# Linear attention with a gated feed-forward on one core: q times k'v in four 64x64 quarters of the TensorE array

## The chip, the cores and the metric

One core of one Trainium2 chip. The metric is the device time of one execution in microseconds (us), lower is better; the time before is the median of three runs. Engines: PE is TensorE's matmul, PEld its weight loads (they overlap PE), DVE is VectorE, ACT ScalarE, POOL GpSimd, SP SyncE, which here only issues DMAs.

## What is computed

Eight batches, eight heads, 576 tokens, 64 channels a head. The attention is linear: softmax of q over its channels, softmax of k over the tokens, and the 64x64 product k'v in between; no score matrix. Behind it stands a gated layer over all 512 channels: a causal depthwise convolution of five taps makes the gate, a product with w_val makes the value, and gate times value goes through w_out. All in fp32.

```python
q_s = np.exp(q - np.max(q, axis=-1, keepdims=True))
q_s = q_s / (np.sum(q_s, axis=-1, keepdims=True) + 1e-09)
k_s = np.exp(k - np.max(k, axis=2, keepdims=True))
k_s = k_s / (np.sum(k_s, axis=2, keepdims=True) + 1e-09)
kv = np.einsum('bhsd,bhse->bhde', k_s, v)
x = np.einsum('bhsd,bhde->bhse', q_s, kv)          # then heads side by side: (8, 576, 512)
for j in range(5):
    gate_pre += conv_w[j] * xp[:, j:j + S, :]      # xp: x with four zero rows ahead
out = (1.0 / (1.0 + np.exp(-gate_pre)) * (x @ w_val)) @ w_out
```

## The kernel before, in words

The work goes batch by batch, and within a batch by *pairs of heads* p (128 channels, so 4 pairs) or by chunks of 128 tokens. A batch has these steps, each a small function:

- **q** (lines 357 to 397): q_max, q_sub, q_exp, q_sum, q_mul make the softmax with tokens on the partitions. In batches 0 and 1 q_each does the subtraction and the exponential per head on ScalarE for some chunks. q_turn (435) transposes q on TensorE, eight blocks of 128x128 into one PSUM buffer; q_turned (446) copies two pairs to the tile qT, with the channels of a pair on the partitions. The 64 tokens left over by the four chunks are turned for two batches together (tail_turn, tail_turned, tail_high, lines 458 to 470).
- **k** (278 to 350): the maximum over tokens comes from a second copy of k with channels on the partitions (k_peak, 283); it goes through DRAM (k_row, k_spread) to be spread over the partitions, then k_sub, k_exp, kt_exp. Batches 0 and 1 use k_top, k_raise and transposes (k_turn) instead.
- **k'v** (kv, 399): for each pair and each of five chunks of tokens one fp32 product per head, 128 tokens by 64 channels, into rows 0 to 63 or 64 to 127 of PSUM: the two heads use the two halves of the array's columns. kv_sums and kv_norm (414, 419) divide by the sums; kv_norm runs once per half and writes into the diagonal blocks of a 128x128 tile kvd whose other blocks are zero.
- **x = q times k'v** (attend, 476): per pair of heads one product over the full array, in two halves of 288 tokens. In batches 0 and 1 (F32_BATCHES) q and kvd are fp32. In the others they are split into high words (fp32r, a reduced format that TensorE takes in one pass) and low words: kv_high and kv_low (427, 431) split kvd, q_turned writes the high words of q, q_low and tail_low (454, 472) the low ones into the buffers "under"; attend then makes three products, low by high, high by high, high by low, in one accumulation.
- **the gated layer** (491 to 564): x_high and x_low split x the same way; first and four tap steps on VectorE form the gate from x in PSUM; a tap can instead be a far on ScalarE (the product) and a near on GpSimd (the addition). sigmoid, then value (546), 24 products over the full array for one block of 128 channels, gated, g_high, g_low, project (562), again 24 products, copy, put.

PSUM is four buffers of two banks each (psum, bank, 157), shared by all transposes, k'v, x, value and project; x of a pair stays in its buffer until its taps and x_low are done. At the start each slab of the two weights arrives as 64-bit words and is turned to fp32 by integer steps (load_words to w_low, lines 225 to 274).

What sets the order is the list ORDER (lines 30 to 143, 1011 steps), written out by hand: each engine, and SP's DMA queue, does its instructions in the order in which they stand there. A last letter a, v or p puts a step on ScalarE, VectorE or GpSimd. The buffers of a tag are taken in turn as they come free, so a load that stands early in the list waits on SP until its buffer is free, with all loads behind it.

## Time and profile before

| | us |
|---|---|
| median of 3 runs | 305.2 (304.4 to 305.86) |
| the profiled execution, its own time | 305.72 |
| its span in the profile | 303.9 |
| TensorE busy | 279.1 (92%) |
| VectorE busy | 255.5 (84%) |
| GpSimd busy | 220.4 (73%) |
| ScalarE busy | 216.2 (71%) |

A span is what the profile covers of one execution. Busy time counts an engine's instructions, overlaps once; TensorE's products are pipelined and their ends are modelled, so durations of single products are longer than their spacing, and the rate is read from how many start in a stretch. An fp32 product shows as two records, one pass with the low words of the weights and one with the high words; an fp32r product shows as one. The chain of waits follows the work that ended last back to what released each piece.

### The profile page before, as it was taken

How to read it: one execution, taken by the hardware profiler on the slowest of the kernel's cores; microseconds unless marked ns; L12 is line 12 of the kernel's file. 1: busy time of each engine (PE TensorE's matmuls, PEld its weight loads, DVE VectorE, ACT ScalarE, POOL GpSimd, SP SyncE). 2: the span in 40 equal slices, each digit the busy share in tenths (PEclk: the TensorE clock that was granted, in tenths of full speed). 3: DMA queues.
4: the chain of work that ended last, by engine and by line, in shares of the span. 5: the costliest groups of instructions: out<-in, count | busy, mean ns of one | idle time of the engine just before them, and what ended most of it. 6: DMA issues, size and time to landing. Idle time of an engine off the chain costs nothing.

```text
span 303.9 us, 6467 instructions
## 1 busy us (share of the span) xinstructions
PE 279.1 (92%) x2536; PEld 271.1 (89%) x2536; DVE 255.5 (84%) x350; ACT 216.2 (71%) x357; POOL 220.4 (73%) x206
## 2 busy tenths in 40 slices
PE   0347899999999899999999999999999999999995
PEld 0336699999989799999999999999998999999995
DVE  3999999999999798999999898999779876836611
ACT  3999999967795996869673964659496885464220
POOL 4677959799989699659787879784886949752500
PEclk9978999999999999999999999999999999999999
DMA  7999491389598822618597099023201210021012
GB/s 240 408 405 396 156 397 45 103 187 361 194 319 261 327 102 75 217 54 284 158 395 304 39 259 332 17 90 106 38 0 39 80 41 0 2 116 41 0 62 96
DMA packets 17454, 51.25 MB, mean 169 GB/s; under 512 B 2705, under 2 KB 3089, under 8 KB 14737
## 3 DMA queue, kind: packets, MB, share of 16 engines
q1 hardware_dynamic: 17424, 50.85, 47.9%
q8 instruction: 20, 0.33, 0.5%
q14 instruction: 10, 0.07, 0.1%
HBM read 41.39 MB, written 9.45 MB: 167 GB/s over the span
## 4 chain that ended last, share of the span: by engine, by line
PE 66%; ACT 11%; DVE 10%; DMA 7%; issue 2%; POOL 2%; SPq 1%; ACTq 0%; DVEq 0%
PE out L534 26%; PE val L534 25%; PE x L487 7%; PE kv L407 4%; PE qTps L439 3%; DVE qs L377 3%; DMA q<-in_q 3%; DMA words<-in_w_val 2%; ACT q L392 2%; DMA out<-o 2%; DVE qm L361 1%; ACT L523 1%; DVE qs L378 1%; ACT qT L171 1%; DVE gate L511 1%
## 5 line engine op out<-in xcount | busy, mean ns | idle before, releaser
L534 PE MATMUL val<-x,w_val_hi 128*128 128x288 f32 x512 | 88.4, 294 | 0.0
L534 PEld LDWEIGHTS val<-x,w_val_hi 128*128 128x128 f32 x512 | 74.8, 188 | 0.0
L511 DVE SCALAR_TENSOR_TENSOR gate<-x,cw,gate 128x573 f32<-128x573 f32 (+3 forms) x91 | 72.1, 807 | 2.2 <-ACT gate L500 1.2
L520 POOL TENSOR_TENSOR gate<-gate,far 128x572 f32<-128x572 f32 (+3 forms) x37 | 49.5, 1341 | 27.3 <-ACT far L516 26.4
L534 PE MATMUL out<-gh,w_out_lo 128*128 128x288 f32 x256 | 55.9, 297 | 1.1 <-ACT o L171 0.6
L534 PE MATMUL val<-x,w_val_lo 128*128 128x288 f32 x256 | 56.0, 299 | 0.0
L534 PE MATMUL out<-gh,w_out_hi 128*128 128x288 f32 x256 | 55.0, 294 | 0.0
L534 PEld LDWEIGHTS out<-gh,w_out_lo 128*128 128x128 f32 x256 | 41.2, 188 | 2.1 <-ACT o L171 0.9
L534 PEld LDWEIGHTS val<-x,w_val_lo 128*128 128x128 f32 x256 | 40.7, 188 | 0.7 <-DVE x L173 0.2
L534 PEld LDWEIGHTS out<-gh,w_out_hi 128*128 128x128 f32 x256 | 41.2, 188 | 0.0
L560 POOL TENSOR_TENSOR gl<-g,gh 128x576 fp32r<-128x576 f32 x24 | 34.6, 1449 | 7.2 <-ACT gh L171 5.0
L534 PE MATMUL out<-gl,w_out_hi 128*128 128x288 f32 x256 | 39.2, 294 | 0.0
L516 ACT ACTIVATE far<-x,cw 128x572 f32<-128x572 f32 (+3 forms) x37 | 27.0, 745 | 13.7 <-DVE gate L511 6.7
L534 PEld LDWEIGHTS out<-gl,w_out_hi 128*128 128x128 f32 x256 | 35.7, 188 | 0.0
L552 DVE TENSOR_TENSOR g<-val,gate 128x576 f32<-128x576 f32 x32 | 24.0, 751 | 10.0 <-PE val L534 5.8
L366 POOL TENSOR_TENSOR q<-q,qm 128x512 f32<-128x512 f32 x29 | 31.0, 1086 | 0.7 <-issue 0.7
L171 ACT COPY o<-out 128x576 f32<-128x576 f32 x27 | 17.2, 637 | 16.7 <-PE out L534 11.5
L301 POOL TENSOR_TENSOR k<-k,kmax 128x512 f32<-128x512 f32 x21 | 28.6, 1377 | 0.1
L506 DVE TENSOR_TENSOR x<-x,x 128x576 fp32r<-128x576 f32 x32 | 23.2, 747 | 6.3 <-ACT far L516 4.1
L523 ACT ACTIVATE gate<-gate 128x576 f32<-128x576 f32 x32 | 21.1, 685 | 8.4 <-DVE gate L511 5.4
L394 POOL TENSOR_TENSOR q<-q,qs 128x512 f32<-128x512 f32 x25 | 26.0, 1048 | 0.8 <-DVE qs L379 0.6
L500 ACT ACTIVATE gate<-x,cw 128x576 f32<-128x576 f32 x27 | 19.9, 747 | 6.8 <-PE x L487 5.2
(88 smaller groups left out, 522.1 us busy)
## 6 DMA issues: line engine op xcount, KB each, us to landing
out<-o SPq DMA_DIRECT2D x31, 288.0 KB, 2.2
v<-in_v SPq DMA_DIRECT2D x8, 1040.0 KB, 8.9
...
```

The source lines that it names most:

```text
L301: engine(e).tensor_sub(kk[r, cs], kk[r, cs], mx[r, cs])
L366: engine(e).tensor_tensor(qq, qq, m, op=ALU.add if b < 2 else ALU.subtract)
L394: engine(e).tensor_mul(qq, qq, s.unsqueeze(2).broadcast_to([P, H, D]))
L487: nc.tensor.matmul(T["x", b, p][:, cs], a, z[:, cs], start=(i == 0), stop=(i == len(parts) - 1))
L506: nc.vector.tensor_sub(xl, T["x", b, p], T["xh", b, p].bitcast(F32))
L511: nc.vector.scalar_tensor_tensor(out=a, in0=x, scalar=w, in1=a, op0=ALU.mult, op1=ALU.add)
L516: nc.scalar.activation(T["far", b, p, j], T["x", b, p][:, :S - n], AF.Copy, scale=cw[:, p, j:j + 1])
L520: nc.gpsimd.tensor_add(a, a, T["far", b, p, j])
L523: nc.scalar.activation(T["gate", b, p], T["gate", b, p], AF.Sigmoid)
L534: nc.tensor.matmul(ps[:, cs], a[:, kb, ms], z[:, cs], start=(i == 0), stop=(i == len(parts) - 1))
L552: nc.vector.tensor_mul(T["g", b, m], T["val", b, m], T["gate", b, m])
L560: engine(e).tensor_sub(T["gl", b, m], T["g", b, m], T["gh", b, m].bitcast(F32))
```

## The change

q times k'v is done in fp32 in all batches, per head, on a quarter of the array: 64 rows by 64 columns. A step attend b g takes two pairs of heads, so four heads, and two PSUM buffers; it makes eight products, one for each head and each half of the tokens, in such an order that four consecutive ones fall on the four quarters. So that this is possible, the heads of every odd pair are exchanged in q (on the host, where the inputs are laid out) and in kv (the line `hd = 2 * p + (h + p) % 2`). The tile kvd has no zero blocks any more, and kv_norm is one instruction for both halves. kv_high, kv_low, q_low and tail_low fall away. The addition of the epsilon and the reciprocal come out of q_sum as steps of their own, q_eps (on any engine) and q_rec. The buffers of tag "f" go from 3 to 6, and the two slabs of words that shared the buffers "under" get buffers "late".

ORDER is new in whole, 959 steps. By kind: attend 32 to 16, kv_norm 16 to 8, far and near 37 to 25 each, tap 91 to 103, q_low 12, tail_low 12, kv_high 6 and kv_low 6 to none, q_eps and q_rec 10 each new; all loads, transposes, value and project in the same number as before. Steps change engines too: g_low on GpSimd 24 to 19, q_turned on VectorE 3 to 6, q_sub on VectorE 3 to 6, g_high on VectorE 5 to 9, first on VectorE 5 to 8. The order of the first 100 steps or so is close to the old one; further on value and project of different blocks change places. Functions and an input that the diff adds but that no step uses (load_qc, q_total, q_log, l_turn, l_row, l_spread, l_sub, c_exp) are left out below, as is the list.

```diff
-KM = 3
-F32_BATCHES = (0, 1)
+STAGED = 6
...
-        place = ("under", 2) if i in (4, 5) else ("pair", 6)
+        place = ("late", 2) if i in (4, 5) else ("pair", 6)
...
-        s = T["qs", b][:, cs]
-        nc.vector.tensor_reduce(out=s, in_=qq, axis=AX.X, op=ALU.add)
-        nc.vector.tensor_scalar_add(s, s, EPS)
+        nc.vector.tensor_reduce(out=T["qs", b][:, cs], in_=qq, axis=AX.X, op=ALU.add)
+
+    def q_eps(b, c0, c1, e="v"):
+        s = T["qs", b][:, heads(b, c0, c1)[1]]
+        if e == "a":
+            nc.scalar.activation(s, s, AF.Copy, bias=EPS)
+        elif e == "p":
+            nc.gpsimd.tensor_scalar(s, s, EPS, 0.0, op0=ALU.add, op1=ALU.add)
+        else:
+            nc.vector.tensor_scalar_add(s, s, EPS)
+
+    def q_rec(b, c0, c1):
+        s = T["qs", b][:, heads(b, c0, c1)[1]]
         nc.vector.reciprocal(s, s)
...
-                    hd = 2 * p + h
+                    hd = 2 * p + (h + p) % 2
...
-    def kv_norm(b, h, e="v"):
-        acc, s, r = T["kv", b], T["ks", b], slice(h * D, (h + 1) * D)
+    def kv_norm(b, e="v"):
+        acc, s = T["kv", b], T["ks", b]
+        t = T["kvd", b] = small.tile([P, NB, D], F32, tag="kvd", name=f"kvd_{b}")
         if e == "v":
-            nc.vector.tensor_mul(kvd[b % 2][r, :, r], acc[r, :, :D], s[r].unsqueeze(2).broadcast_to([D, NB, D]))
+            nc.vector.tensor_mul(t, acc[:, :, :D], s.unsqueeze(2).broadcast_to([P, NB, D]))
         else:
             for p in range(NB):
-                nc.scalar.mul(kvd[b % 2][r, p, r], acc[r, p, :D], s[r, p:p + 1])
+                nc.scalar.mul(t[:, p], acc[:, p, :D], s[:, p:p + 1])
...
-            T["qT", b] = work.tile([P, NB, S], F32 if b in F32_BATCHES else F32R, tag="qT", name=f"qT_{b}")
+            T["qT", b] = work.tile([P, NB, S], F32, tag="qT", name=f"qT_{b}")
...
-    def attend(b, p):
-
-        T["x", b, p] = halved_bank(f"x_{b}_{p}")
-        qh = T["qT", b][:, p]
-        if b in F32_BATCHES:
-            parts = ((kvd[b % 2][:, p], qh),)
-        else:
-            hi, lo = (T["kvs", b][:, i, p * P:(p + 1) * P] for i in range(2))
-            parts = ((lo, qh), (hi, qh), (hi, T["qTlo", b, p // 2][:, p % 2]))
-        for i, (a, z) in enumerate(parts):
-            for cs in tokens("a"):
-                nc.tensor.matmul(T["x", b, p][:, cs], a, z[:, cs], start=(i == 0), stop=(i == len(parts) - 1))
+    def attend(b, g):
+
+        kvb, qb = T["kvd", b], T["qT", b]
+        for p in (2 * g, 2 * g + 1):
+            T["x", b, p] = halved_bank(f"x_{b}_{p}")
+        for z in range(2):
+            for h in range(2):
+                for p in (2 * g, 2 * g + 1):
+                    cs = tokens("a")[(z + h) % 2]
+                    i, o = (slice(y * D, (y + 1) * D) for y in (h, (h + p) % 2))
+                    nc.tensor.matmul(T["x", b, p][o, cs], kvb[i, p], qb[i, p, cs], start=True, stop=True)
...
-    kvd = [const.tile([P, NB, P], F32, tag=f"kvd{i}", name=f"kvd{i}") for i in range(2)]
+    lses = [const.tile([P, 64], F32, tag=f"lse{i}", name=f"lse{i}") for i in range(2)]
     ktz = [const.tile([P, C], F32, tag=f"ktz{i}", name=f"ktz{i}") for i in range(2)]
+    eps = const.tile([P, 1], F32, tag="eps", name="eps")
+    nc.gpsimd.memset(eps, EPS)
     nc.scalar.preload_act_table(AF.Exp)
-    for t in kvd + ktz:
+    for t in ktz + lses:
...
+    q = np.asarray(q)[:, [h ^ (h // 2 % 2) for h in range(H)]]
     (qm, qt), (km, kt), (vm, vt) = tokens(q), tokens(k), tokens(v)
```

## Rows read from the trace of the kernel before

**Rows 1.** The page: busy time of each engine, its share of the span and its instructions; and the granted TensorE clock in 40 slices of 7.6 us, in tenths of full speed.

```profile
PE 279.1 (92%) x2536; PEld 271.1 (89%) x2536; DVE 255.5 (84%) x350; ACT 216.2 (71%) x357; POOL 220.4 (73%) x206
PEclk9978999999999999999999999999999999999999
```

**Rows 2.** Busy time of each engine by stretch of the span, with the number of instructions in brackets, then the granted clock, the DMA engines' share and GB/s.

```profile
20.00:40.00 20.00, 15.90 (x213) 13.37 (x212) 19.54 (x37) 19.27 (x41) 15.18 (x16) 0.86 0.81 304
40.00:78.00 38.00, 38.00 (x285) 36.79 (x282) 37.17 (x50) 33.44 (x60) 32.94 (x28) 1.00 0.65 221
78.00:110.00 32.00, 30.43 (x286) 29.20 (x282) 29.71 (x40) 26.24 (x46) 27.17 (x25) 1.00 0.74 250
110.00:180.00 70.00, 70.00 (x716) 69.19 (x715) 65.95 (x88) 52.39 (x80) 57.76 (x55) 1.00 0.55 186
180.00:260.00 80.00, 79.30 (x726) 78.31 (x726) 69.02 (x91) 55.03 (x78) 60.52 (x54) 1.00 0.24 82
260.00:300.00 40.00, 39.96 (x303) 39.73 (x302) 18.98 (x27) 15.41 (x24) 14.49 (x13) 1.00 0.13 49
```

**Rows 3.** Pieces of the chain that ended last, in order of time: start, length, engine, tile, line, count.

```profile
36.40 1.24 PE x L487 x4
37.64 2.48 PE kv L407 x80
53.98 0.87 PE qTps L439 x8
54.85 1.94 PE x L487 x8
118.46 3.17 PE val L534 x24
121.63 0.79 PE x L487 x6
289.26 11.39 PE out L534 x84
300.68 0.46 DVE o L173
```

**Rows 4.** Groups of instructions with their shapes: the products of q and k'v (line 487). After the bar: busy us, mean ns of one, idle time of the engine before them and what ended it.

```profile
L487 PE MATMUL x<-qT,kvs 128*128 128x288 f32 x96 | 16.8, 296 | 0.8 <-ACT o L171 0.8
L487 PE MATMUL x<-qTlo,kvs 128*128 128x288 f32 x48 | 10.3, 297 | 0.2 <-DVE qTlo L456 0.2
L487 PE MATMUL x<-qT,kvd 128*128 128x288 f32 x32 | 9.1, 417 | 1.4 <-ACT k L171 0.8 <-ACT qT L171 0.5
```

**Rows 5.** The instructions in order of time, merged, at the start of k'v of batch 3 (line 407): one row of each of three answers, cut at 110.80, 110.88 and 110.91 us. Start, length, engine, line, operation, shapes, count.

```profile
110.78 0.28 PE L407 MATMUL kv<-v,k 128*64 128x65 f32 x2
110.78 0.20 PEld L407 LDWEIGHTS kv<-v,k 128*64 128x64 f32 x4 [0.16 <-POOL gate L520]
110.78 0.34 PE L407 MATMUL kv<-v,k 128*64 128x65 f32 x4
```

**Rows 6.** The same view, TensorE alone, around that k'v: the end of the value product before it, its last two fifths and the start of the value product behind it.

```profile
109.76 1.09 PE L534 MATMUL val<-x,w_val_hi 128*128 128x288 f32 x7
...
112.00 0.64 PE L407 MATMUL kv<-v,k 128*64 128x65 f32 x16
112.58 0.64 PE L407 MATMUL kv<-v,k 128*64 128x65 f32 x16
113.26 0.54 PE L534 MATMUL val<-x,w_val_lo 128*128 128x288 f32 x2
113.64 0.43 PE L534 MATMUL val<-x,w_val_hi 128*128 128x288 f32 x2
```

**Rows 7.** Groups of the page and of VectorE's own list: taps, subtractions for the low words of q, normalization of k'v, the addition of the epsilon. Columns as in group 4.

```profile
L511 DVE SCALAR_TENSOR_TENSOR gate<-x,cw,gate 128x573 f32<-128x573 f32 (+3 forms) x91 | 72.1, 807 | 2.2 <-ACT gate L500 1.2
L456 DVE TENSOR_TENSOR qTlo<-qTps,qT 128x1024 fp32r<-128x1024 f32 x12 | 14.4, 1218 | 2.7 <-ACT qT L171 2.6
L422 DVE TENSOR_TENSOR kvd<-kv,ks 64x256 f32<-64x256 f32 x13 | 5.5, 422 | 0.3
L378 DVE TENSOR_SCALAR qs<-qs 128x16 f32<-128x16 f32 (+3 forms) x10 | 4.9, 495 | 0.3
```

**Rows 8.** Groups of the page on GpSimd and ScalarE: gate additions, low words of g, and the products handed to GpSimd.

```profile
L520 POOL TENSOR_TENSOR gate<-gate,far 128x572 f32<-128x572 f32 (+3 forms) x37 | 49.5, 1341 | 27.3 <-ACT far L516 26.4
L560 POOL TENSOR_TENSOR gl<-g,gh 128x576 fp32r<-128x576 f32 x24 | 34.6, 1449 | 7.2 <-ACT gh L171 5.0
L516 ACT ACTIVATE far<-x,cw 128x572 f32<-128x572 f32 (+3 forms) x37 | 27.0, 745 | 13.7 <-DVE gate L511 6.7
```

**Rows 9.** The instructions in order of time: VectorE, the low words of x for two pairs of heads of batch 1; TensorE, the start of value 1 1.

```profile
68.89 1.54 DVE L506 TENSOR_TENSOR x<-x,x 128x576 fp32r<-128x576 f32 x2
...
71.29 0.42 PE L534 MATMUL val<-x,w_val_lo 128*128 128x288 f32 x2
```

**Rows 10.** Waits of TensorE, and of its weight loads: us in total, times, longest.

```profile
PE x L487 <- ACT o L171: 0.8, 1, 0.8
PE x L487 <- DVE qTlo L456: 0.2, 1, 0.2
PEld x L487 <- DVE qTlo L456: 0.5, 1, 0.5
```

More of the change, by code (lines that the diff above doesn't have):

```diff
@@ new lines @@
+    far 1 2 0, tap 1 1 0, q_sub 2 2 p, sigmoid 1 0, x_low 1 2, sigmoid 1 1, w_low 7 v, copy 0 2 a a, q_sub 2 4 v,
+    put 0 2, q_sub 2 1 p, tap 1 2 3, load_km 4 0, load_km 4 2, x_low 1 3, value 1 1, k_sub 2 1 p, q_exp 2 0 5,
+    tap 1 2 2, value 1 0, gated 1 1, k_sub 2 2 p, tap 1 2 1, first 1 3 a, q_sum 2 0 5, k_sub 2 0 p, k_sub 2 3 p,
+    project 0 3, near 1 2 0, tap 1 3 3, q_eps 2 0 5 a, k_exp 2, q_rec 2 0 5, gated 1 0, q_mul 2 3 p, value 1 3,
+    k_sub 2 4 v, q_mul 2 4 p, q_max 3 0 4, kt_exp 2, copy 0 3 a a, g_high 1 1 p, g_high 1 0 a, q_mul 2 0 p, q_mul 2 2 a,
@@ new lines @@
+    load_km 5 1, load_q 5 0 5, g_high 2 2 p, g_high 2 1 a, q_turned 3 1 a, tap 2 3 1, g_low 2 2 p, q_turned 3 0 v,
+    far 2 3 0, near 2 3 0, attend 3 0, gated 2 0, q_sub 4 0 p, k_peak 6 0, value 2 3, x_high 3 0 a, k_peak 5 3,
+    sigmoid 2 3, g_high 2 0 p, first 3 0 v, far 3 1 0, g_low 2 1 p, tap 3 0 3, tap 3 0 2, g_low 2 0 p, q_exp 4 0 5,
+    gated 2 3, g_high 2 3 v, g_low 2 3 v, project 2 1, tap 3 0 1, first 3 1 a, far 3 1 2, x_low 3 0, project 2 0,
+    copy 2 1 a a, tap 3 0 0, put 2 1, tap 3 1 3, q_sum 4 0 5, near 3 1 2, attend 3 1, k_sub 4 4 p, copy 2 0 a a,
@@ new lines @@
+    x_low 4 2, x_low 4 3, q_mul 5 3 p, sigmoid 4 0, value 4 0, first 4 2 a, first 4 3 v, q_mul 5 0 p, kv_sums 5,
+    tap 4 3 3, q_mul 5 1 p, kv_norm 5 v, far 4 3 2, k_peak 6 3, q_sub 6 0 p, tap 4 2 3, k_row 6, load_k 6, near 4 3 2,
+    value 4 2, tap 4 2 2, tap 4 2 1, tail_high 5 p, q_sub 6 3 p, k_spread 6, tap 4 2 0, put 3 2, gated 4 0, load_vt 6,
+    sigmoid 4 2, tap 4 3 1, q_turn 5 0, sigmoid 4 1, g_high 4 0 p, g_low 4 0 p, tap 4 3 0, value 4 1, gated 4 2,
+    sigmoid 4 3, q_turned 5 0 a, k_sub 6 2 p, q_turn 5 1, gated 4 1, g_high 4 2 p, attend 5 0, k_sub 6 1 p,
@@ new lines @@
+    load_q 7 0 5, q_turned 5 1 v, value 4 3, q_sub 6 4 p, first 5 1 v, first 5 0 a, tap 5 0 3, far 5 1 0, g_high 4 1 p,
+    far 5 1 2, g_low 4 1 v, x_high 5 1 a, g_low 4 2 v, x_high 5 0 a, gated 4 3, g_high 4 3 v, tap 5 1 3, q_exp 6 0 5,
+    g_low 4 3 p, project 4 0, q_max 7 0 4, near 5 1 2, project 4 1, copy 4 0 a a, k_sub 6 4 p, x_low 5 1, put 4 0,
+    tap 5 1 1, k_sub 6 0 p, k_peak 7 3, tap 5 0 2, attend 5 1, copy 4 1 a a, k_sub 6 3 p, tap 5 0 1, project 4 2,
+    first 5 2 a, tap 5 0 0, near 5 1 0, far 5 3 1, x_low 5 0, q_sum 6 0 5, far 5 2 3, x_high 5 2 a, near 5 2 3,
@@ new lines @@
+    kt_exp 6, project 4 3, q_sub 7 0 p, far 5 2 2, copy 4 2 a a, x_low 5 2, q_eps 6 0 5 a, put 4 2, q_rec 6 0 5,
+    put 4 1, q_mul 6 1 p, sigmoid 5 0, q_sub 7 1 p, x_high 5 3 a, sigmoid 5 1, x_low 5 3, value 5 1, near 5 2 2,
+    copy 4 3 a v, first 5 3 a, q_mul 6 0 p, put 4 3, tap 5 2 1, value 5 2, load_v 6, k_peak 7 2, q_mul 6 2 p, k_exp 6,
+    tap 5 2 0, q_mul 6 4 p, tap 5 3 3, q_mul 6 3 p, tap 5 3 2, value 5 0, gated 5 1, near 5 3 1, k_peak 7 0,
+    g_high 5 1 a, g_low 5 1 p, tap 5 3 0, sigmoid 5 2, tail_turn 6, q_sub 7 2 p, gated 5 0, sigmoid 5 3, q_turn 6 0,
@@ new lines @@
+    gated 5 2, g_high 5 0 a, q_sub 7 3 p, q_turn 6 1, g_low 5 0 p, kv 6, q_turned 6 1 v, q_exp 7 0 4, q_turned 6 0 v,
+    value 5 3, g_high 5 2 a, q_sum 7 0 4, tail_turned 6 a, tail_high 6 p, kv_sums 6, kv_norm 6 v, g_low 5 2 v,
+    attend 6 0, gated 5 3, g_high 5 3 p, first 6 0 a, x_high 6 1 v, far 6 0 3, g_low 5 3 p, project 5 0, k_peak 7 1,
+    x_low 6 1, k_row 7, first 6 1 v, near 6 0 3, tap 6 1 3, project 5 3, copy 5 0 a a, tap 6 1 2, k_spread 7,
+    q_eps 7 0 4 a, put 5 0, tap 6 1 1, tap 6 1 0, attend 6 1, copy 5 3 a a, put 5 3, project 5 2, x_high 6 3 a,
@@ new lines @@
+    put 5 2, tap 6 3 1, sigmoid 6 2, kv 7, tap 6 3 0, gated 6 2, sigmoid 6 3, g_high 6 2 v, value 6 3, kv_sums 7,
+    q_turned 7 0 v, kv_norm 7 v, q_turn 7 1, gated 6 3, attend 7 0, g_high 6 3 v, g_low 6 2 v, g_low 6 3 p, project 6 1,
+    far 7 0 1, x_high 7 1 v, q_turned 7 1 a, x_low 7 1, first 7 1 v, first 7 0 a, x_high 7 0 a, x_low 7 0, project 6 0,
+    tap 7 1 3, far 7 0 2, copy 6 1 a a, tap 7 0 3, put 6 1, near 7 0 2, project 6 3, near 7 0 1, far 7 1 0,
+    copy 6 0 a a, tap 7 0 0, attend 7 1, copy 6 3 a a, far 7 1 1, put 6 3, project 6 2, first 7 2 v, put 6 0,
@@ L278, in load_km @@
     def load_km(b, j):
[L280 removed]
+        t = T["km", b, j] = block("f", f"km_{b}_{j}", STAGED)
         nc.sync.dma_start(out=t, in_=km[b, j])
```

247 lines of the change are left out of this document (117 added, 130 removed).

## The prediction

> **What bounds the kernel now.** I read the table of engines first, then the busy time by stage, then the chain that ended last. TensorE is busy for 92% of the span, VectorE for 84% [rows 1]. By stage it is plainer [rows 2]: from 40 us on TensorE is full (38.00 us of 38.00, then 70.00 of 70.00, 79.30 of 80.00, 39.96 of 40.00), and only the stretch from 78 to 110 us has holes, 1.6 us of 32. VectorE is nearly as full up to 78 us (19.54 of 20, 37.17 of 38) and has a quarter or more to spare only behind 180 us, about half behind 260. ScalarE and GpSimd have room from 40 us on. The chain says the same [rows 3]: small pieces by turns on VectorE, ScalarE and TensorE up to 40 us, then one run of TensorE to the last product at 300.7 us, and a copy and a store behind it. So a microsecond of TensorE work taken out behind 40 us is a microsecond of time, as long as VectorE can follow; VectorE is the engine to watch up to about 80 us. The granted clock is at full speed from 30 us on and falls only between 20 and 30 us [rows 1], where TensorE mostly waits for others; nothing below hangs on it.
>
> **TensorE, what goes.** In batches 2 to 7 a pair of heads costs six one-pass products of 288 columns, 0.79 us in the chain [rows 3]; four pairs, 3.16 us; six batches, 19.0 us. In batches 0 and 1 a pair has two fp32 products of two passes each, four records [rows 4]; the chain has two pairs in 1.94 us [rows 3], so 0.243 us a pass over 288 columns and 3.88 us a batch, 7.8 us for two. In all 26.8 us go.
>
> **TensorE, what comes.** Sixteen blocks (two a batch), each eight fp32 products of 64 rows by 64 columns over 288 tokens, two passes each. One quarter gets two products in a block, four passes: 4 x 0.243 = 0.97 us if the four quarters run side by side. No row shows a product of 64 rows, so I bound it. Below: 0.97. Above: all 16 passes in a row, 3.89 us. In between, two at a time, 1.94. The nearest row is k'v, which runs on halves of the columns [rows 5]: its 80 passes of 65 columns take 2.48 us, 31 ns each, while a pass of 65 columns at the rate above (0.243 x 65/288) takes 55 ns. Two therefore run at once. More than that: the first two passes of the block start within 20 ns of each other with the same duration, and two more start by 110.91 us. In program order the two passes of one half (low words of the weights, then high words) stand next to each other, and two passes of one half cannot stream together. So the array looked past the waiting second pass to the other half. With that, four quarters side by side is what I take: 0.97.
>
> The Trainium skill, "TensorE: Matmul & The Clock Gate", Part 3 on packing small matmuls, says against this that matmuls start and end strictly in program order and that only weight loads are pulled ahead. By that rule the high pass of a quarter holds up the next quarter, only two passes overlap, and a block would take some 2.2 us instead of 0.97; it is the slower rival below.
>
> To this comes the change of the array's shape. Around k'v it can be read [rows 6]: the last full-array product starts at 110.55 (109.76 and six steps of 0.132), the next would start at 110.69, k'v starts at 110.78; its 40 pairs (ten in 0.58, from 112.00 to 112.58) would end at 113.10, the next full-array product starts at 113.26, and its successors come 0.12 late. Together 0.09 + 0.16 + 0.12 = 0.37 us a block. It could be less (below: 0.1, if the longer passes cover it). I take 0.37: a block is 1.34 us, sixteen 21.4 us. **TensorE saves 26.8 - 21.4 = 5.4 us.** The transposes, value, project and k'v keep their counts.
>
> **VectorE.** Gone: twelve subtractions for the low words, 1.22 us each, 14.6; thirteen half normalizations of k'v become five whole ones at the same 0.42 us, -3.4; eight of ten small additions of the epsilon, 0.5 each, move to ScalarE and GpSimd, -3.9 [rows 7]. With the low words of k'v and some smaller moves (words, copies, tails) about 31 us go. Come: twelve more taps at 0.81, 9.7 us [rows 7], since twelve far/near pairs fall away; and steps taken over from the others (g_low, q_turned, q_sub, g_high, first), some 18 us. Net -2 to -3 us of 255.5: VectorE is not relieved, it only does other work. **GpSimd** loses twelve gate additions (1.34), five g_low (1.45), and all low words of kv and of the tails, about 35 us net; **ScalarE** twelve far at 0.75, copies and q_mul heads, about 19 us net [rows 8]. Neither was the bound, so this pays nothing directly.
>
> **Where VectorE catches TensorE.** I added up the mean durations in the order of the two step lists. Up to the end of x_low 1 3 VectorE has 69.3 us of work before and 69.8 after; before, that step ends at 70.4 us (the pair of steps that starts at 68.89) [rows 9], so after at about 70.8. Value 1 1, which needs it 22 products (2.9 us) after its own start, has 46.6 us of TensorE work ahead of it before and 41.1 after (project 0 3 now stands behind it, and four cheaper blocks ahead). Value 1 1 started at 71.29 [rows 9], so TensorE ran 24.7 us behind its own work; as late as that it would be there at 65.8 and want the data at 68.7: it waits about 2.1 us. Against this stand the holes of 78 to 110 us, 1.6 us [rows 2]; among their causes the waits for the low words, 0.2 on products and 0.5 on weight loads, cannot come back [rows 10], and TensorE now arrives there later relative to VectorE. I count 1.3 us of them as gone.
>
> **Queues, buffers, ends.** No DMA is added or dropped by count: the new load of q by channels is in no step. On SP's queue loads move: v of batch 1 goes out earlier, since it takes a free buffer instead of k'v 0's; v of batch 2 goes out later, after q of batch 3, and its cover is the work up to k'v 2; if that cover is gone, k'v 2, q's transposes and all products behind them wait, for up to the length of one load. A block takes two of the four PSUM buffers at once where a pair took one; the price is a wait for a tap or a copy, of the size of the 0.8 us that products already wait for o [rows 10]. One memset more on GpSimd lies in the first microseconds, ahead of any data. The end stays: last product, half a copy, a store.
>
> **Sum.** The profiled execution took 305.7 us around a span of 303.9, 0.5 above the median of the runs. 305.7 - 5.4 + 2.1 - 1.3 = 301.1, less 0.5 for the median: **300.5 us**.
>
> **Rivals.**
> Two quarters at a time (slower). Place: every block. For it: no row has products of different rows together, and the program order of the passes. Against: [rows 5]. Price: a block is 1.94 + 0.37 = 2.31 us, sixteen 37.0, so +10.2 instead of -5.4: about 315 us; with strict order, 8 x 0.243 + 0.243 + 0.37 = 2.56 a block, 41.0, about 319. It decides from a block of 1.68 us on (26.8 / 16). Chance 0.13.
> VectorE or the buffers eat it. If VectorE holds TensorE up for twice the 2.1 us and more, as it idled 7.2 us itself between 40 and 180 us [rows 2], or if blocks wait 0.3 us each for their two buffers (16 x 0.3 = 4.8), the 5.4 are gone: 304 to 306. For it: VectorE has no room to 78 us [rows 2]. Against: from 180 us on it idles 11 us of 80 [rows 2], and the other engines hand it its data with less to do. Chance 0.12.
> The change of shape is hidden and the waits of VectorE vanish: 16 x 0.27 = 4.3 more, about 296. For it: a pass of 288 columns is long against a load of weights. Against: [rows 6], where full-array products behind k'v come late. Chance 0.10.
> Forecast: 0.65, between 298 and 303.5.
>
> **How the numbers follow.** About 0.5% (1.5 us) is what a measurement can tell from no change. Faster by more: the forecast and the third rival, 0.75. Within 0.5%: most of the second, 0.10. Slower: the first and a rest, 0.15. The range 295.5 to 306.5 takes in all but the first rival and leaves out under 2 in 10.
>
> **What would show it.** Right: a block of 32 passes in about 1 us of starts, four starts close together, and about 1.3 us from the full-array product before to the one behind; TensorE still full from 40 us; VectorE the releaser of a wait around 65 to 75 us; GpSimd near 185 us busy, VectorE near 253. Wrong: starts in twos 0.24 us apart, blocks over 1.7 us; or TensorE with many holes behind 80 us, ended by VectorE or by copies that free PSUM; or k'v 2 released by the load of v.

## The result: 306.5 us, and the profile after

306.5 us median, against 305.2 for the kernel before beside it; the ratio is 1.0061, 95% interval 1.0031 to 1.009. (Medians are of all runs; ratios, here and below, are of the means of the fast runs, those within 1.5% of the kernel's fastest.) The forecast was 300.5, so the change is slower by about half a per cent where it was to be 1.5% faster. The profiled execution of after took 308.5 us, 2.0 above the median of its runs, and its span is 306.7; that of before took 305.7 around 303.9 [rows 1].

The table of engines, to be read beside [rows 1]:

```profile
PE 277.0 (90%) x2616; PEld 257.9 (84%) x2616; DVE 253.6 (83%) x339; ACT 199.1 (65%) x328; POOL 189.8 (62%) x177
```

Every engine has less to do, GpSimd 30.6 us less and ScalarE 17; TensorE's busy time falls by 2.1 only. Busy time by stage says where the time is; columns as in [rows 2]:

```profile
20.00:40.00 20.00, 14.24 (x164) 10.80 (x166) 19.14 (x31) 17.23 (x42) 16.46 (x20) 0.76 0.65 255
40.00:78.00 38.00, 36.24 (x331) 33.39 (x330) 36.80 (x49) 30.16 (x57) 30.67 (x27) 1.00 0.64 239
78.00:110.00 32.00, 31.09 (x309) 28.97 (x308) 28.73 (x38) 23.03 (x36) 24.17 (x23) 1.00 0.71 235
110.00:180.00 70.00, 68.63 (x724) 64.48 (x723) 64.94 (x82) 50.49 (x79) 46.78 (x41) 1.00 0.55 193
180.00:260.00 80.00, 79.19 (x743) 75.07 (x744) 66.93 (x90) 48.99 (x63) 50.74 (x45) 1.00 0.26 84
```

In [rows 2] TensorE filled the stretches 40 to 78 and 110 to 180 us without a hole. Here 1.8 and 1.4 us are missing there. The holes of 78 to 110 us were 1.6 and are still 0.9. Behind 260 us TensorE is full. VectorE has about the work of before in each stage up to 180 us.

A block of q times k'v, in order of time on TensorE: the last full-array products ahead of it, its 16 passes (eight products of two passes each; the prediction's last part wrote 32 by a slip), the first one behind.

```profile
234.62 1.23 PE L572 MATMUL out<-gl,w_out_hi 128*128 128x288 f32 x8
235.78 1.20 PE L525 MATMUL x<-qT,kvd 64*64 64x288 f32 x16
236.91 0.53 PE L572 MATMUL out<-gh,w_out_lo 128*128 128x288 f32 x2
```

The last full-array product ahead starts at 235.55 (234.62 and seven steps of 0.133), the first one behind at 236.91, and its successor comes 0.24 late instead of 0.13. The block costs 1.33 us; it was forecast at 1.34. Twelve of the 16 blocks go like this one; the other four stand in the start or wait inside or ahead of the block.

So the price of a block is the forecast one, and by it 5.4 us go out of TensorE's work. What took them back is seen in four views. First, the full-array products. Each chain of waits has one run of 96 products of value near its end; the row of before, then that of after:

```profile
274.94 12.69 PE val L534 x96
```

```profile
277.24 12.80 PE val L572 x96
```

0.11 us over 95 steps is 1.16 ns a product: 132.2 ns apart before (12.69 us over 96), 133.3 after. A kernel has 1,536 of them, in all stages, so about 1.8 us.

Second, the start. The pieces of TensorE from the second block on, and then busy time by stretch, where the third column from the end is the granted clock:

```profile
36.45 2.79 PE L525 MATMUL x<-qT,kvd 64*64 64x288 f32 x16 [0.26 <-ACT k L166]
39.18 1.04 PE L466 MATMUL kv<-v,k 128*64 128x65 f32 x16
...
42.01 0.53 PE L572 MATMUL val<-x,w_val_lo 128*128 128x288 f32 x2
```

```profile
34.00:36.00 2.00, 0.46 (x5) 0.42 (x4) 2.00 (x5) 2.00 (x4) 0.66 (x2) 1.00 0.00 0
36.00:38.00 2.00, 1.74 (x12) 0.95 (x13) 2.00 (x4) 1.95 (x5) 1.84 (x3) 0.64 0.00 0
38.00:40.00 2.00, 2.00 (x27) 1.06 (x21) 1.65 (x5) 1.08 (x4) 1.59 (x2) 0.50 0.00 0
```

k'v 1 starts at 39.18 us; before it started at 37.64 [rows 3], with 1.2 us more work ahead of it. Value 0 0 starts at 42.01. From 36 to 38 us the clock is at 0.64 and from 38 to 40 at 0.50, so at the lower of its two levels (1.2 GHz) most of the time, after TensorE had been busy 0.46 of two microseconds. From the start of this block to value 0 0 it takes 5.56 us; in a_noeps below, at full clock, 4.61. This loss belongs to the execution that was profiled, which is one of the long ones.

Third, TensorE's waits behind 40 us (us in total, times, longest):

```profile
PE x L525 <- DVE gate L549: 1.0, 1, 1.0
PE val L572 <- ACT qT L166: 0.9, 1, 0.9
PE qTps L491 <- issue: 0.8, 1, 0.8
PE val L572 <- DVE x L544: 0.8, 1, 0.8
PE kv L466 <- ACT k L305: 0.7, 1, 0.7
PE x L525 <- ACT kvd L485: 0.4, 1, 0.4
```

None is long, but they are 4.8 us, where before had 2.1. In order of time: at 65 us attend 1 1, for the PSUM buffer of its second pair, which a tap frees; at 74 value 1 1, for x_low; at 90 value 1 2, for a buffer that ScalarE's copy of q's transposes frees; at 116 k'v 3, for the exponential of k; at 161 attend 4 0, for the normalization of k'v; at 253 q_turn 7 0. Each is a single step that comes late. ScalarE is the last releaser of three (value 1 2, k'v 3, attend 4 0), and ahead of each of them it had itself waited for VectorE (1.5, 1.1 and 4.8 us). For k'v 3, VectorE first, then ScalarE:

```profile
110.00 2.81 DVE L361 TENSOR_REDUCE qm<-q 128x40 f32<-128x2560 f32 x1
112.73 0.92 DVE L301 TENSOR_TENSOR k<-k,kmax 128x512 f32<-128x512 f32 x1
...
113.71 1.28 ACT L305 ACT_TABLE_LOAD   x1 [1.08 <-issue]
```

VectorE does q's maximum of a later batch ahead of k_sub 3 2, which ends at 113.65; ScalarE, idle for 1.08 us, then starts on the exponential that k'v 3 waits for.

Fourth, the end. Before copies the left half of the last output ahead of project 7 3's right half, and behind the last product VectorE copies the right half alone, 0.46 us [rows 3]. After copies both halves behind it, on ScalarE:

```profile
302.99 0.70 ACT L166 COPY o<-out 128x288 f32<-128x288 f32 x2 [2.59 <-PE out L572]
```

From the start of the last product (300.35 before, 302.62 after) to the end of the span it is 3.53 us before and 4.07 after. In b_quarters below, which has the change's functions and the last copies of before, it is 3.53.

### The profile page after: what moved, and what is told of

It is laid out like the page before. It is cut to its first block, busy times and chain, and to the rows that moved or that the text cites. A ratio compares the mean times of both kernels' runs of the same rounds, so it can differ in the third digit from the quotient of the medians.

```text
span 306.7 us, 6523 instructions
## 1 busy us (share of the span) xinstructions
PE 277.0 (90%) x2616; PEld 257.9 (84%) x2616; DVE 253.6 (83%) x339; ACT 199.1 (65%) x328; POOL 189.8 (62%) x177
## 4 chain that ended last, share of the span: by engine, by line
PE 60%; DVE 15%; DMA 12%; ACT 6%; issue 4%; SPq 1%; POOL 0%; ACTq 0%; DVEq 0%
PE out L572 26%; PE val L572 23%; DMA kc<-in_k_channels 5%; PE x L525 5%; DVE gate L549 4%; PE kv L466 3%; DMA q<-in_q 3%; PE qTps L491 2%; DMA km<-in_k_strided 2%; DVE kpk L286 2%; DVE g L590 1%; DVE qs L376 1%; DVE qm L361 1%; DMA words<-in_w_out 1%; DVE x L544 1%
## 5 line engine op out<-in xcount | busy, mean ns | idle before, releaser
L549 DVE SCALAR_TENSOR_TENSOR gate<-x,cw,gate 128x575 f32<-128x575 f32 (+3 forms) x103 | 81.7, 806 | 4.7 <-POOL gate L558 3.4
L558 POOL TENSOR_TENSOR gate<-gate,far 128x572 f32<-128x572 f32 (+3 forms) x25 | 34.3, 1374 | 37.5 <-DVE gate L549 19.6
L572 PE MATMUL out<-gh,w_out_lo 128*128 128x288 f32 x256 | 56.9, 301 | 0.0
L598 POOL TENSOR_TENSOR gl<-g,gh 128x576 fp32r<-128x576 f32 x19 | 29.3, 1547 | 24.3 <-DVE gh L168 18.4
L166 ACT COPY o<-out 128x576 f32<-128x576 f32 (+1 forms) x30 | 18.5, 622 | 34.4 <-PE out L572 27.8
L453 POOL TENSOR_TENSOR q<-q,qs 128x512 f32<-128x512 f32 x28 | 29.2, 1060 | 6.4 <-DVE qs L389 6.2
L301 POOL TENSOR_TENSOR k<-k,kmax 128x512 f32<-128x512 f32 x19 | 25.4, 1345 | 6.8 <-DMA kmax<-krow 6.8
L366 POOL TENSOR_TENSOR q<-q,qm 128x512 f32<-128x512 f32 x26 | 27.7, 1078 | 0.8 <-issue 0.5
L554 ACT ACTIVATE far<-x,cw 128x572 f32<-128x572 f32 (+3 forms) x25 | 18.5, 744 | 11.8 <-PE x L525 6.6
L466 PE MATMUL kv<-v,k 128*64 128x65 f32 x512 | 21.8, 237 | 3.1 <-DMA v<-in_v 2.4
```

What stands on the lines that cost most here:

```text
L166: nc.scalar.copy(out=out, in_=in_)
L301: engine(e).tensor_sub(kk[r, cs], kk[r, cs], mx[r, cs])
L366: engine(e).tensor_tensor(qq, qq, m, op=ALU.add if b < 2 else ALU.subtract)
L453: engine(e).tensor_mul(qq, qq, s.unsqueeze(2).broadcast_to([P, H, D]))
L466: nc.tensor.matmul(acc[h * D:(h + 1) * D, p, :], T["k", b][:, c, cs] if c < 4 else ktz[b % 2][:, cs], T["v", b][:, c, hd] if c < 4 else T[ ...
L549: nc.vector.scalar_tensor_tensor(out=a, in0=x, scalar=w, in1=a, op0=ALU.mult, op1=ALU.add)
```

## Experiments

All kernels of one call ran beside the kernel before on the same chip; medians of before were 304.9 to 305.4. Ratios are to before.

### Is it the place in SBUF, the order, or the start?

**a_noeps**: after without the tile that no step reads.

```diff
-    eps = const.tile([P, 1], F32, tag="eps", name="eps")
-    nc.gpsimd.memset(eps, EPS)
```

> The changed kernel without the tile eps and its memset, which no step reads; every tile behind it in SBUF lies 32 bytes lower, as in the kernel before. Theory A (the place of the tiles in SBUF slows the full-array products: 133.35 ns apart after, 132.19 before): they are 132.2 ns apart again, 1536 x 1.17 ns = 1.8 us less, about 304.7 us. Rival (the spacing comes from what runs beside the products, the new mix of work on VectorE and GpSimd): the spacing stays 133.3 and the time 306.5.

Measured: 305.23 us, 1.0011 (0.9991 to 1.0032). The 96 products of value:

```profile
274.54 12.69 PE val L572 x96
```

**b_pad**: the kernel before with such a tile.

```diff
     ktz = [const.tile([P, C], F32, tag=f"ktz{i}", name=f"ktz{i}") for i in range(2)]
+    pad = const.tile([P, 1], F32, tag="pad", name="pad")
+    nc.gpsimd.memset(pad, EPS)
```

> The kernel before with one unused tile of 4 bytes a partition and its memset put where the change puts eps, so that the tiles behind it lie 32 bytes higher. Theory A: products 133.3 ns apart instead of 132.2, about 1.8 us more, 307.0 us, with the order and the steps of before. Rival: 132.2 and 305.2, no change.

Measured: 306.36 us, 1.0041 (1.0026 to 1.0056).

```profile
274.94 12.80 PE val L534 x96
```

Theory A is shown from both sides: 12.69 without the tile and 12.80 with it, in either order of steps. What moves, by 32 bytes, is what is allocated behind the constants, x, g and q among it; the weights stand ahead of it and stay. So the 1.3 us between the medians of after and before (1.1 in b_pad) are a tile of four bytes a partition that nothing reads. Why this place is slower, no run shows. The change of q times k'v itself comes out at no change, 4.7 us above the forecast.

**b_quarters**: the blocks in the order of before.

```diff
-    q_sum 2 0 5, ..., kv_norm 2 1 v, ..., kv_norm 2 0 v, ..., kv_high 2 a, ..., kv_low 2 p, ..., tail_low 2 0 p, ..., q_low 2 0,
-    ..., attend 2 0, ..., attend 2 1, q_low 2 1, ..., tail_low 2 1 p, ..., attend 2 3, ..., attend 2 2, ...
+    q_sum 2 0 5, q_eps 2 0 5 v, q_rec 2 0 5, ..., kv_norm 2 v, ..., attend 2 0, ..., attend 2 1, ...
```

> The change's functions in the order of before: each block stands where the first of its two pairs stood, kv_norm where its first half stood, the steps for the low words of q and k'v and of the tails are dropped, q_eps and q_rec stand right behind q_sum on VectorE; no eps tile. Theory B (TensorE's 5.4 us are there, and the new order gives them back in waits and in slower products): VectorE keeps its 12 far/near pairs on the other engines and loses about 31 us of work, so it follows; 5.4 us less than before, 299 to 301 us. Rival C (blocks of four heads cost more than their products: both PSUM buffers at once, x of two pairs needed together, or the start): the waits come here too, 304 us or more.

Measured: 315.19 us, 1.0255 (1.0204 to 1.0306), so 7.8 us more by the ratio, although VectorE has 237 us of work instead of 255.5. At 98 us, TensorE alone:

```profile
97.92 1.67 PE L524 MATMUL x<-qT,kvd 64*64 64x288 f32 x16
102.50 0.54 PE L571 MATMUL out<-gh,w_out_lo 128*128 128x288 f32 x2 [2.91 <-ACT o L165]
...
103.62 0.68 PE L571 MATMUL out<-gh,w_out_hi 128*128 128x288 f32 x2
```

Behind a block, which has just taken two of the four PSUM buffers, project 1 1 waits 2.91 us for one that a copy of ScalarE frees. Then full-array products start 0.24 us apart instead of 0.13, up to about 106 us: the clock has fallen to its lower level (0.68 granted from 104 to 108 us). Such a wait comes once more at 176 us (2.4, for x_low). Rival C holds and theory B as put falls: in the order of before the blocks cost about 8 us.

**a_start**: a_noeps with another start.

```diff
-    k_turned 1 0 a, q_turn 0 1, first 0 1 a, ..., scaled 2 v, signed 2, x_high 0 1 a, x_high 0 0 v, x_low 0 0, k_raise 1 2, ...
+    k_raise 1 2, k_turned 1 0 a, q_turn 0 1, ..., q_turned 0 1 a, x_high 0 0 v, x_low 0 0, k_turned 1 1 a, ..., attend 0 1, x_high 0 1 a, ..., scaled 2 v, signed 2, ...
```

> As a_noeps, with the steps between k_turned 1 0 and attend 0 1 put in another order: on ScalarE q_turned 0 1, k_turned 1 1 and k_tail_turned 1 ahead of first and x_high, on VectorE k_raise 1 2, x_high 0 0 and x_low 0 0 ahead of scaled 2 and signed 2. Value 0 0 starts at 42.0 us after and at 40.0 before. Theory D (what is lost at the start stays lost, TensorE being full behind it): value 0 0 comes 1 to 3 us earlier and the end with it, 302 to 303.5 us. Rival (VectorE sets the pace up to about 75 us, so that an earlier start only lengthens the wait at attend 1 1 and value 1 1): the time of a_noeps, 304.7.

Measured: 309.05 us, 1.013 (1.011 to 1.0151). The order was badly chosen, and the trace of VectorE says how:

```profile
30.28 0.76 DVE L166 CAST x<-x 128x576 fp32r<-128x576 f32 x1 [1.79 <-PE x L523]
...
35.36 0.82 DVE L547 SCALAR_TENSOR_TENSOR gate<-x,cw,gate 128x575 f32<-128x575 f32 x1 [3.52 <-ACT x L164]
```

The integer steps for the weights had filled two waits of VectorE, 1.79 and 3.52 us. Behind those waits they now came late. k'v 1 slipped from 37.78 us in a_noeps to 41.45, value 0 0 from 40.66 to 45.39, and the end by 3.9 us (spans 303.8 and 307.7). So a delay at the start does reach the end, most of it (3.9 of 4.7 us); that part of theory D stands, though not by the sign that was wanted.

### Is it a handful of late steps?

**a_five**: a_noeps with five steps moved, one for each wait.

```diff
-    ..., value 3 2, gated 3 3, tail_high 4 p, q_sub 5 3 p, k_peak 6 1, g_high 3 3 a, kv_norm 4 a, ...
+    ..., value 3 2, kv_norm 4 a, gated 3 3, tail_high 4 p, q_sub 5 3 p, k_peak 6 1, g_high 3 3 a, ...
-    ..., copy 1 2 a a, k_sub 3 2 v, value 2 2, ...
+    ..., attend 2 1, k_sub 3 2 p, q_rec 3 0 4, ...
-    ..., k_sub 7 3 p, ..., k_sub 7 2 v, k_sub 7 0 v, value 6 2, ...
+    ..., k_sub 7 0 v, k_sub 7 3 p, ..., k_sub 7 2 v, value 6 2, ...
...
```

> a_noeps (305.2 us) with five steps moved in the list, each of which, or whose engine, releases a wait of TensorE in the trace of a_noeps: kv_norm 4 five steps earlier on ScalarE (attend 4 0 waits 0.6 for it), k_sub 7 0 nine steps earlier on VectorE (q_turn 7 0 waits 0.9 for a PSUM buffer whose taps stand behind it), k_sub 3 2 from VectorE to GpSimd and 26 steps earlier (kv 3 waits 0.9 for k_exp 3), sigmoid 1 2 twenty steps earlier (value 1 2 waits 0.9 for q_turned 2 0, behind the switch of ScalarE's table), q_sum 7 0 six steps later (behind attend 6 0's kv_norm 6). Theory E (the 5.4 us of TensorE went into a handful of steps that stand late in the list, with room beside them): adding up the measured durations in the new order gives 5.0 us less, 300.2 us. Rival (VectorE is the bound up to 180 us, so what one wait gives back the next one takes): under half of it, 303 us or more.

Measured: 303.28 us, 0.9927 (0.9901 to 0.9952): 2.0 us less than a_noeps, not 5.0. TensorE's longest waits behind 40 us, first in a_noeps, then here:

```profile
PE x L525 <- DVE gate L549: 1.0, 1, 1.0
PE val L572 <- ACT qT L166: 0.9, 1, 0.9
PE kv L466 <- ACT k L305: 0.9, 1, 0.9
PE qTps L491 <- issue: 0.9, 1, 0.9
PE x L525 <- ACT kvd L485: 0.6, 1, 0.6
```

```profile
PE val L570 <- ACT qT L164: 1.4, 1, 1.4
PE val L570 <- DVE x L542: 0.6, 1, 0.6
```

Of the five rows above, four are gone (k'v 3, q_turn 7 0, attend 4 0, and attend 1 1, which no move was meant for), and one for x_low at value 1 1 is new. That for qT is longer: ScalarE now waits 1.4 us for the store of an earlier output before it copies the next (0.2 in a_noeps), and sigmoid 1 2, which was moved up, comes on top of it. Behind value 0 0 the profiled execution is 3.4 us shorter than that of a_noeps (255.65 us from there to the last product against 259.07); 1.1 of it is lost ahead, where no step was moved (value 0 0 at 41.79 against 40.66, the clock at 0.58 and 0.57 from 36 to 40 us). Theory E is right in kind and too large in size.

**a_thirteen**: eight more.

```diff
-    load_km 4 1, far 1 2 0, tap 1 1 0, ..., project 0 3, near 1 2 0, ...
+    load_km 4 1, tap 1 1 0, ..., project 0 3, far 1 2 0, g_high 1 1 p, near 1 2 0, ...
-    project 7 2, copy 7 0 a a, put 7 0, project 7 3 l, ...
+    project 7 3 l, put 6 2, project 7 2, copy 7 0 a a, put 7 0, ...
...
```

> a_five with eight more steps moved (g_high 1 1, g_high 1 0 to VectorE, w_high 7 from GpSimd to ScalarE, k_peak 2 1, tap 2 0 1, q_mul 2 1, far 1 2 0, and the first half of project 7 3 ahead of project 7 2). Theory E: 1.9 us more, 298.4 us. Rival: as a_five.

Measured: 305.32 us, 1.0001 (0.9977 to 1.0024), so 2.0 more than a_five. A miss for theory E; the profiled execution was 4.6 us above the median, so no cause is read from it.

**a_order**: some 600 moves, of which two places.

```diff
-    attend 1 1, copy 0 1 a a, q_sub 2 3 p, x_low 1 1, k_spread 2, ...
+    attend 1 1, w_low 6 p, q_sub 2 1 p, tap 1 1 2, load_k 4, ...
-    k_sub 7 2 v, k_sub 7 0 v, value 6 2, g_low 6 0 p, tap 6 2 2, ...
+    tap 6 2 2, k_sub 7 3 p, k_sub 7 0 p, value 6 2, ...
...
```

> a_noeps with the list behind value 0 0 worked over in some 600 small moves, each kept when the durations added up in that order came out lower (also with 5% on those of VectorE, ScalarE and GpSimd); no function is changed. Theory E: 7.8 us less than a_noeps by that sum, 297.5 us, TensorE without a wait over 0.3 us behind 45 us. Rival: 302 us or more, since the durations of VectorE and GpSimd grow where more of them lie side by side.

Measured: 315.47 us, 1.0275 (1.0219 to 1.0331), 16 us above the sum by the ratio and 18 by the median. TensorE at attend 1 1, then busy time, clock and DMA share in the stretches around it:

```profile
63.97 0.69 PE L523 MATMUL x<-qT,kvd 64*64 64x288 f32 x2
67.70 1.20 PE L523 MATMUL x<-qT,kvd 64*64 64x288 f32 x14 [3.04 <-DVE gate L547]
...
69.73 0.68 PE L570 MATMUL out<-gh,w_out_lo 128*128 128x288 f32 x2
```

```profile
64.00:67.70 3.70, 0.67 (x3) 0.16 (x2) 3.70 (x7) 0.64 (x1) 3.62 (x4) 1.00 0.07 18
...
68.80:72.50 3.70, 3.70 (x19) 3.67 (x17) 2.88 (x5) 3.56 (x6) 1.42 (x3) 0.54 0.92 381
```

The first row holds two passes, those of the first product alone: its quarter starts the second at 64.27, 0.29 us behind the first. The other 14, the next of which needs the second buffer, come after 3.04 us of waiting. Then the clock is at 0.54 for 3.7 us and full-array products start 0.24 us apart. The wait costs 3.0 us, and the slow 16 products behind it another 1.6.

**a_orderb**: the same order with the four buffers written out.

```diff
-        return psum.tile([P, 2 * 512], F32, tag="bank", name=name)
+        return psum.tile([P, 2 * 512], F32, tag="bank" + next(BANKS), name=name)
...
```

> a_order (315.5 us, where the sum of durations gives 297) with the four PSUM buffers taken as written in a list, in each place the one that comes free first by that sum; order and steps are those of a_order. Theory I (the build fixes which buffer a tile gets before any time is known; in a_order x 1 3 and out 1 2 got one that came free 2 to 3 us later than another, TensorE stood for 3.0 us, and its clock fell to half for the next 3.6 us): most of the 18 us come back, 300 us or less. Rival (the durations on VectorE and GpSimd grow where they lie side by side, or the loads come late): 310 us or more.

Measured: 312.1 us, 1.0234 (1.0187 to 1.0281). The medians differ by 3.4 us, a fifth of the 18, the ratios by 1.3, and the intervals overlap; theory I falls as the main cause. For the rival's late transfers the trace has this: GpSimd waits 13.9 us for the spread maxima of k (6.0 in a_noeps) and ScalarE 6.8 for stores of outputs (0.2 in a_noeps), both on SP's queue. That these make up the rest was not tested, and such waits alone don't make a slow kernel: a_mv21b below, which is faster than before, has 7.8 and 4.5.

```profile
POOL k L304 <- DMA kmax<-krow: 13.9, 4, 4.7
```

```profile
ACT o L169 <- DMA out<-o: 6.8, 2, 4.6
```

**a_mv21b**: 21 moves, each also good with 5% longer durations, and buffers written out.

```diff
-    ..., copy 1 2 a a, k_sub 3 2 v, value 2 2, ...
+    ..., project 1 1, k_sub 3 2 v, copy 1 0 a a, ...
-    ..., k_sub 7 2 v, k_sub 7 0 v, value 6 2, ...
+    ..., k_sub 7 0 v, copy 5 2 a a, ...
...
```

> a_noeps with 21 steps moved or given to another engine, chosen one after the other by adding up the measured durations (also with 5% more on VectorE, ScalarE and GpSimd), among them those of a_five in kind: k_sub 3 2 and k_sub 7 0 earlier, sigmoid 1 2 and q_mul 2 2 earlier, q_sum 7 0 later. Beside it the four PSUM buffers are taken as written in a list (in each place the one that comes free first by that sum) instead of as the build chooses. Theory E (waits on steps that stand late, in the reach of the list): 6.6 us less by the sum, about 299 us. Rival (VectorE has no room up to 90 us): as a_five or worse, 303 us or more.

Measured: 301.96 us, 0.9889 (0.9874 to 0.9904). It beats the kernel before by 3.4 us and the changed one by 4.5.

```profile
78.00:110.00 32.00, 31.75 (x311) 29.27 (x310) 29.73 (x39) 24.87 (x38) 26.81 (x24) 1.00 0.73 248
110.00:180.00 70.00, 69.64 (x735) 65.42 (x734) 65.49 (x86) 50.20 (x79) 49.28 (x43) 1.00 0.51 184
180.00:260.00 80.00, 80.00 (x764) 75.45 (x763) 67.77 (x90) 49.28 (x63) 48.41 (x43) 1.00 0.25 84
```

```profile
PE x L528 <- DVE gate L552: 2.1, 2, 1.9
```

From 78 to 260 us TensorE now has 0.6 us of holes; after had 3.1. VectorE has as much work there as in after. The one wait of any size left is at attend 1 1, for its second buffer. Part of the gain lies ahead of these stretches: two of the 21 moves stand ahead of value 0 0 (one takes q_eps 1 2 4 from ScalarE to GpSimd), TensorE's wait there for ScalarE's copy of qT falls from 1.55 to 0.56 us, and value 0 0 comes at 39.60 us (40.66 in a_noeps). Of the 2.9 us between the two spans 1.1 are there and 1.9 behind value 0 0.

**a_mv21**: the same 21 moves, buffers as the build chooses.

```diff
-        return psum.tile([P, 2 * 512], F32, tag="bank" + next(BANKS), name=name)
+        return psum.tile([P, 2 * 512], F32, tag="bank", name=name)
...
```

> a_mv21b with the PSUM buffers as the build chooses them. If the choice of buffers matters (theory I, of which a_orderb showed 3.4 us): 1 us more or above, 303 us. Rival (in this order both choices free in time): 302.0 us.

Measured: 302.58 us, 0.9914 (0.9883 to 0.9946). The intervals overlap; in this order the choice of buffers can't be told from nothing, and the gain is the order's.

### Where is TensorE the bound?

**a_twice01** and **a_twice67**: a_noeps with the products of the blocks of two batches issued twice (the edit of a_twice01; the other has `b > 5`).

```diff
-        for z in range(2):
+        for z in range(4 if b < 2 else 2):
```

> a_noeps (305.2 us) with the eight products of a block issued twice in batches 0 and 1 (the second time over the same values), four blocks: 16 more passes each, 0.97 us, so 3.9 us more work for TensorE up to 67 us. Theory H (up to about 90 us the time is not set by TensorE, so the 2.4 of the 5.4 us that the change takes out of batches 0 and 1 were never on the path): under 2 us more, 307 us or less. Rival (TensorE is the bound from 40 us on, as the prediction had it): the two blocks behind 40 us cost all of their 1.9 us and those of the start part of theirs, 3 to 4 us more, 308.5 to 309 us.

> The same in batches 6 and 7: four blocks, 3.9 us more work for TensorE behind 225 us. Theory H: TensorE is the bound there, all of it is paid, 309.1 us. Rival (TensorE's waits behind 225 us, 0.9 for q_turn 7 0 among them, take some of it up): 307.5 us or less.

Measured: 306.43 us, 1.0043 (1.0021 to 1.0065), and 309.6 us, 1.0131 (1.0116 to 1.0146). The same 3.9 us of TensorE work cost 1.2 us in batches 0 and 1 (1.0 by the ratios) and 4.4 in batches 6 and 7 (3.7 by the ratios). Theory H holds in both halves. Two of the four blocks of batches 0 and 1 stand ahead of 40 us, so the 1.2 are not of the stretch behind 40 us alone; batches 2 to 5 were not doubled.

**a_taps01** and **a_mvtaps**: less work for VectorE instead, from a_noeps and from a_mv21b. Both leave out one tap of the gate in batches 0 and 1.

```diff
-    tap 0 1 1, ..., tap 0 0 1, ..., tap 1 3 1,
```

> a_noeps without one of the five taps (j = 1) in batches 0 and 1: eight taps of 0.81 us, 6.5 us less work for VectorE up to about 90 us; the gate of those batches lacks that term. Theory J (VectorE is short of time up to 90 us, and that alone makes TensorE late there): TensorE's waits at 64 us (1.15) and those of its start shrink, the later ones stay; 2 us less or more, 303.2 us at most. Rival (up to 115 us the next wait hangs on another chain, the maxima and exponentials of k on ScalarE and GpSimd, and takes back what VectorE gives): 1 us less, 304.2 us or more.

> The same eight taps left out of a_mv21b (301.96 us), where the later waits are gone and TensorE's one long wait behind 40 us is 1.9 at the second buffer of attend 1 1, ended by a tap. Theory J: that wait goes and nothing takes it up, 1.5 to 3 us less, 299 to 300.5 us. Rival: under 0.7 us less.

Measured: 304.75 us, 0.9999 (0.9978 to 1.0019), and 301.25 us, 0.9879 (0.9849 to 0.9909). Eight taps are 6.5 us of VectorE, and they bring 0.5 and 0.7 us in the medians, within the intervals. Theory J falls: the longest wait at attend 1 1 does shrink, from 1.9 us in a_mv21b to 1.0 in a_mvtaps, but the time hardly moves. So up to about 90 us neither TensorE's nor VectorE's amount of work sets the time by itself. What does was not isolated; that it is the run of small dependent steps over ScalarE, VectorE, GpSimd and the loads at the start, with the k of batches 2 and 3 behind, is argued from a_start, and from the start of a_mv21b.

### Do the quarters depend on the order of the products?

**a_rows**: the four passes of a quarter stand in a row.

```diff
-        for z in range(2):
-            for h in range(2):
-                for p in (2 * g, 2 * g + 1):
+        for h in range(2):
+            for p in (2 * g, 2 * g + 1):
+                for z in range(2):
```

> a_noeps with the eight products of a block in another order: the two halves of the tokens of one head follow each other, so four passes in a row go to the same quarter instead of two. Theory F (TensorE looks past the waiting passes of a quarter, however many): the block stays at 0.97 us of starts and 1.33 us from the full-array product before to the one behind, 305.2 us. Theory G (it looks past one waiting pass only, which in the order of the change is all that stands in the way): a quarter's second product waits and holds the next quarter up, a block takes about twice as long, 1.9 to 2.3 us; sixteen of them, 15 us more, 320 us.

Measured: 305.51 us, 1.001 (0.9988 to 1.0032).

```profile
233.83 1.22 PE L525 MATMUL x<-qT,kvd 64*64 64x288 f32 x16
234.98 0.53 PE L572 MATMUL out<-gh,w_out_lo 128*128 128x288 f32 x2
```

The block takes as long as in the order of the change, 1.15 us from its first start to the next full-array product against 1.13. Sixteen starts come in fours, 13 ns apart within a four and 0.24 us from four to four (6 to 7 ns in the order of the change). One quarter alone starts its second pass 0.29 us behind its first (a_order, at 63.97 us), so each four is one pass of each quarter, though four passes of one quarter stand in a row in the program. Theory F holds: TensorE looks past three waiting passes of one quarter. The Trainium skill, "TensorE: Matmul & The Clock Gate", Part 3 on packing small matmuls, has matmuls start and end strictly in program order; for the passes of fp32 products on quarters this trace shows otherwise, and the measurement decides.

## Why the prediction was wrong

**TensorE, what goes and comes: right.** 1.33 us a block against 1.34 forecast, in twelve of 16 blocks, four quarters at once. The first rival (two at a time, 315 us) is out, by a_rows even for the order that would have been worst. The third (change of shape hidden) is out as well: the full-array products behind a block still come late, as in [rows 6].

**The step that failed: "a microsecond of TensorE work taken out behind 40 us is a microsecond of time".** It was read off a busy share of 38.00 in 38.00 and 70.00 in 70.00 [rows 2]. A full TensorE in the trace of before says only that TensorE has no room at today's work. It doesn't say how near the next chains are. The stretch from value 0 0 to the last product, in before and in a_noeps:

```profile
40.05:300.35 260.30, 257.99 (x2304) 253.55 (x2300) 220.78 (x291) 182.46 (x286) 192.88 (x172) 1.00 0.43 145
```

```profile
40.66:299.73 259.07, 254.16 (x2363) 239.46 (x2364) 217.66 (x286) 165.22 (x252) 161.02 (x139) 1.00 0.43 150
```

(Both executions lie 0.3 to 0.5 us above the medians of their runs.) TensorE's work is 3.8 us less there, of the 4.2 that the forecast has there (5.4 less 1.2 of batch 0: 3.88 less 2 x 1.34). But its holes grow from 2.3 to 4.9, so the stretch is shorter by 1.2 us only. Those 1.2 go as well: value 0 0 comes 0.6 us later (40.66 against 40.05), although the 1.2 us of batch 0 were to make it earlier, and the end takes 0.5 more. The forecast booked batch 0's share although its blocks stand ahead of 40 us, outside its own condition.

The doubled blocks say the same by stage. In batches 0 and 1 together, with 2.4 of the 5.4 us, a microsecond of TensorE is worth a third (a_twice01); the forecast had set 2.1 us for one wait of VectorE there. In batches 6 and 7 a microsecond more costs a whole one (a_twice67).

Between, single steps are late that a share of busy time does not show: 1.4 us of holes from 110 to 180 us in after, none before. "As long as VectorE can follow" was read off VectorE's share too. VectorE has the time, but its steps do not end when TensorE needs them: a_mv21b has as much work on VectorE in that stretch (65.49 us, 64.94 in after) and 0.4 us of holes. It brings 3.3 us without touching a product.

**"1.3 us of the holes are gone": not.** 0.7 of the 1.6 us went. What the prediction named as unable to come back (waits for low words) didn't; others took their place, as the rows of waits show.

**VectorE catches TensorE around value 1 1, 2.1 us: right in size, wrong in kind.** The holes from 40 to 78 us are 1.8 us, at attend 1 1 and value 1 1. But over half of it is the wait for the second PSUM buffer, the term that the prediction had priced at 0.8 under buffers and left out of the sum, and less work on VectorE halves that wait without moving the time by more than 0.7 us (a_mvtaps).

**What the prediction didn't have: the tile eps.** It counted the memset and not the shift. 1.3 us, what stands between the medians of the changed kernel and the one before. The page of before could not show it; a reader of the diff could have asked what lies behind a new tile.

**The start, not in the sum.** In the execution profiled, value 0 0 came 2.0 us later than in before (42.01 against 40.05). One of the two is the clock, and a_noeps, with the same order, kept its clock in the execution profiled, though TensorE was about as idle from 34 to 36 us:

```profile
34.00:36.00 2.00, 0.66 (x4) 0.42 (x4) 2.00 (x4) 2.00 (x4) 0.66 (x2) 1.00 0.02 7
...
38.00:40.00 2.00, 2.00 (x76) 2.00 (x74) 2.00 (x5) 1.99 (x4) 1.99 (x2) 1.00 0.05 8
```

In a_rows, the same up to there but for the order within a block, it was at 0.50 from 38 to 40 us. What decides is not settled.

**"The end stays: last product, half a copy, a store": not.** Two half copies on ScalarE in place of one on VectorE, 0.5 us, put at nothing without a look at the last steps of the two lists.

**The outcome was that of the second rival** (the 5.4 are eaten, 304 to 306; 305.2 without the tile), by a part of its cause: from 110 us on not VectorE's fullness, which was its reason, but the places of a few steps on VectorE and ScalarE. It was given 0.12. The forecast's 0.65 rested on [rows 2] without asking which steps had been early by less than a microsecond.

**The sum from 300.5 to 306.5**: 1.3 for the tile (a_noeps), 3.3 for late steps (a_noeps less a_mv21b, a third of it in the start), and 1.4 left, which a_mv21b still has against the forecast. In its trace 0.5 of this is the end (4.06 us from the start of the last product, 3.53 before), and some 0.7 is batch 0, whose 1.2 us bring value 0 0 only 0.45 us earlier (39.60 against 40.05). No run tests these two one by one, and both are read from single executions.

Of the rest: GpSimd came out at 189.8 us busy (forecast near 185), VectorE at 253.6 (near 253). k'v 2 was not released by the load of v.
